# w1's parts loaded and transposed ahead of w_out, a sum of taps split around a tile, and softmax steps moved on ScalarE, in the start-up of a dynamic convolution with a max-out layer

## The chip, the cores and the metric

One core of one Trainium2 chip. The metric is the device time of one execution in microseconds (us), the median over several runs; lower is better. The engines are named as the profile names them: PE (TensorE, matmuls), PEld (its weight loads), DVE (VectorE), ACT (ScalarE), POOL (GpSimd), SP (SyncE, which here only issues DMAs). POOL issues DMAs too.

## The reference, cut to what matters

```python
# x (8, 4160, 192), weight_gen (8, 4160, 8 heads, 7 taps), all float32
w = exp(weight_gen - max); w = w / (sum(w over taps) + 1e-9)      # softmax over 7 taps
x_pad = zeros(6 rows) + x along the sequence
y[b, s, h, :] = sum over k of w[b, s, h, k] * x_pad[b, s + k, h, :]   # 24 channels a head
x2 = y.reshape(33280, 192)
h1 = x2 @ w1; h2 = x2 @ w2                                        # (192, 1024) each
out = maximum(h1, h2) @ w_out                                     # (1024, 192)
```

## The kernel before, in words

**Algebra.** maximum(h1, h2) is h1 + relu(h2 - h1). So the kernel keeps `wd` = w2 - w1 in bf16 for the hidden layer, and a small matrix `w10` = w1 @ w_out for the part without the relu. `w10` is a product that PE makes once (`w10_product`, lines 751 to 762): 8 matmuls with the transposed first 128 rows of w1 (part "E", line 755), then 16 with 64 columns each, which alternate between E and the transposed last 64 rows (part "T", line 759). The transposed parts lie in `w1t`; each is loaded and cast to bf16 by a DMA of POOL (lines 708 and 710) and transposed by a DMA of SP (line 713) that waits for that load. ACT copies the product out of PSUM (lines 766 and 768, `w10_copies`). `wo` is w_out in bf16, loaded by POOL (line 704), first read by the output matmuls of line 402 and then by the product.

**Layout.** The 33280 rows stand as 128 partitions of 260 columns. Columns are taken in batches of 16 (the last has 4). Of a batch, ACT makes exponentials of the logits (`exp_sum`, line 162), DVE their sums (`red`, 180), ACT the logarithms of the sums (`ln`, 186), DVE subtracts them from the logits (`shift`, 191), ACT makes the normalized weights (`weights(b, o)`, 202, o the first column in the batch; in batches 0 and 1 in pieces of 4 columns, two instructions each), and DVE multiplies x by them for all seven taps (`mul(b, o)`, 218, or `mul_pair`, 227) into `m_t`. From batch 2 on DVE adds the taps (`adds`, 244 to 253) and SP transposes the sums `yt` by a DMA (262). In batches 0 and 1, PE adds and transposes at once: `sum_part` (307) makes 84 matmuls of a piece of 4 columns against the identity, in two halves of 42, and ACT copies the result to `yt` (316). `sum_transpose` is both halves, with its copy at once or handed back (`features`).

**Hidden and output layer.** The 130 hidden tiles (1024 numbers in each partition) are made by `hid_tile` (362) and go through ACT's `relu` (372) to bf16. The output matmuls take wo with relu's result (402) and w10 with yt (415, in the start-up 457); ACT copies two or four columns' outputs to `o_t` (`evac`, 487), which SP stores (501). The tiles go in groups: of two up to tile 16 (so groups 0 to 7), of three from there. From group 3 on `hidden` writes out a group: hidden tiles, first half of the outputs of earlier columns, relus, second half, evac, and between them the softmax steps and sums of taps of later columns. A PSUM buffer of two tiles lets tile t + 2 begin when the relu of tile t is done.

**Order.** The schedule is written by hand: each engine runs its instructions in the order of the program text and waits by semaphores, so an instruction that waits holds all that stand behind it on its engine. `behind(first, load)` holds a load back until the instruction `first` is done, and with it all that stands behind the load on POOL. `relay` puts an empty instruction on a queue that waits for PE and that PE then waits for; the first (`out_hidden_only`, 440) is on SP, behind the transposes of w1.

The order around the change: groups 0 to 3 are written out one by one at lines 727 to 800; then `weights(1, 8)` (983), `rest_of_1` (807: the multiply of columns 8 to 11 of batch 1), and the loop over groups. In group 4 the exponential and sums of batch 2 stand behind the second relu (992), `weights(1, 12)` and `ln(2)` behind the output copy (905).

Of the kernel before, what the change touches and what calls it, by code (L numbers as in the profile page):

```python
# [23 lines left out]
def kernel(  # L24
# [9 lines left out]
    nc = tc.nc  # L34
# [3 lines left out]
    F = moe_w1.shape[1]  # L38
    P = 128
# [3 lines left out]
    HF = F // 2  # L43
# [65 lines left out]
    def load_wg(b, eng, o=0, n=None):  # L109
        c0, w = BATCHES[b]  # L110
        if b not in wg_ts:
            wg_ts[b] = pwg.tile([P, w * WGC], FP32, name="wg_t", tag="wg")
        parts = [(o, n)] if n else [(0, 8), (8, 8)] if c0 + w == LAST else [(0, w)]
        for o, n in parts:
            load = eng.dma_start(
                out=wg_ts[b][:, o * WGC:(o + n) * WGC],
                in_=bass.AP(tensor=weight_gen.tensor, offset=actual(c0 + o) * WGC,
                            ap=[[CPP * WGC, P], [1, n * WGC]]),
            )
        return load  # L120
# [9 lines left out]
    def load_x(b, o, n, halo=True):  # L130

        t, at = x_at(b, o)
        load = nc.gpsimd.dma_start(  # L133
            out=t[:, at + PAD * D:at + (PAD + n) * D],
            in_=bass.AP(tensor=x.tensor, offset=actual(BATCHES[b][0] + o) * D,
                        ap=[[CPP * D, P], [1, n * D]]),
        )
        if 0 < b < NB - 1 and o == 0 and halo:
            load_halo(b)
        if "wrap" in xb_ts and t is xb_ts["wrap"]:  # L140
            nc.gpsimd.memset(t[0:1, 0:PAD * D], 0.0)
            nc.gpsimd.dma_start(
                out=t[1:P, 0:PAD * D],
                in_=bass.AP(tensor=x.tensor, offset=(CPP - PAD) * D, ap=[[CPP * D, P - 1], [1, PAD * D]]),
            )
        return load
# [35 lines left out]
    def ln(b, i=0, of=1):  # L182
        if i == 0:
            s_ts[b] = psm.tile([P, BATCHES[b][1] * H], FP32, name="ln_t", tag="ln")
        hs = part(b, i, of)[0]
        nc.scalar.activation(out=s_ts[b][:, hs], in_=sums(b, hs), func=AF.Ln)  # L186
# [7 lines left out]
    def weights(b, o):  # L194

        w = dict(pieces(b))[o]
        if b not in en_ts:
            en_ts[b] = pen.tile([P, 16 * WGC * 2], BF16, name="en_t", tag="en")
        J = 2 if w == 4 and b < 2 else 1
        N = w * H // J  # L200
        for j in range(J):
            nc.scalar.activation(  # L202
                out=_sub(en_ts[b], (o * WGC + j * N * K) * 2, [[2 * N, K], [2, N], [1, 2]]),
                in_=_sub(wg_ts[b], (o * H + j * N) * K, [[1, K], [K, N], [0, 2]]), func=AF.Exp,
            )


    def mul(b, o):

        n = dict(pieces(b))[o]  # L210
        t, at = x_at(b, o)
        if n == 4 and b < 2:
            m_out = _sub(m_t, K * o * D, [[64, 2], [P, K * 6], [1, 64]])
            x_in = _sub(t, at, [[2 * D, 2], [D, K], [1, 2 * D]])
        else:
            m_out = m_t[:, K * o * D:K * (o + n) * D]
            x_in = _sub(t, at, [[D, K], [1, n * D]])
        return nc.vector.tensor_tensor(  # L218
            out=m_out, in0=x_in,
            in1=_sub(en_ts[b], o * WGC * 2, [[2, K * n * H], [0, G // 2], [1, 2]]),  # L220
            op=ALU.mult,
        )
# [56 lines left out]
    def half(j):  # L279
        return slice(64 * j, 64 * j + 64)  # L280
# [4 lines left out]
    def sum_transpose(u, taps=range(K), amid=lambda: None, now=True):  # L285

        copy = sum_part(u, 0, 3, taps)
        amid()
        sum_part(u, 3, 6, taps)
        if now:  # L290
            copy()
        return copy
# [30 lines left out]
    relu_of, yt_of, w10_of = {}, {}, []  # L323

    def behind(first, load):

        tc.add_manual_dep(load.ins, first.ins.name, SYNC, reason="its place among the transfers")
# [26 lines left out]
    def hid_tile(t):  # L354


        u = TILES[t][0]
        fs, w = chunks(t)
        for f in fs:
            for s in range(3):  # L360
                for j in range(2):
                    nc.tensor.matmul(  # L362
                        hid_out(t, f, j), lhsT=wd_at(j, s, f // 4, f % 4 * P, P),
                        rhs=_sub(yt_ts[u][half(j), :], (s + j) % 3 * P, [[3 * P, w // P], [1, P]]),
                        start=(f == fs[0] and s == 0), stop=(f == fs[-1] and s == 2),
                        skip_group_check=True,
                    )

    def relu(rd, t0, n):

        (hd, at), k = hd_at[t0], rd_at[t0][1]
        relu_of[t0] = nc.scalar.activation(out=rd[:, k * 1024:(k + n) * 1024], in_=hd[:, at:at + n * 1024],  # L372
                                           func=AF.Relu)
# [146 lines left out]
    OUTS, c = [[], [], []], 0  # L520
# [31 lines left out]
    def hidden(g, now=(), between=lambda: None, beside=lambda: None, ahead=lambda: None, amid=lambda: None):  # L552


        t0, n = GROUPS[g]
        rd = room(g)
        for t in range(t0, t0 + n - 1):
            hid_tile(t)
        if now:
            out_room(now, "ab" if n == 1 and "ab" in ps else None)  # L560
            last = out_first(now)
        if len(now) > 2:
            relu(rd, t0, n - 1)
        else:
            for t in range(t0, t0 + n - 1):
                relu(rd, t, 1)
        if now:
            go = relay(last)
        amid()
        hid_tile(t0 + n - 1)  # L570
        if len(now) > 2:
            beside()
        relu(rd, t0 + n - 1, 1)
        ahead()
        if now:
            out_second(now, go)
            evac(now[0] // 2, len(now) // 2)
        between()
        if len(now) <= 2:
            beside()  # L580
# [35 lines left out]
    with tc.tile_pool(name="pstage", bufs=1) as pstage:  # L616
# [73 lines left out]
        def halves_swapped(frm, bank):  # L690
# [10 lines left out]
        behind(first_exp, load_x(0, 4, 4))  # L701
        behind(first_mul, load_x(0, 8, 4))
        load_x(0, 12, 4)
        nc.gpsimd.dma_start(
            out=wo[:, :].rearrange("p (f d) -> p f d", d=D),
            in_=bass.AP(tensor=moe_w_out.tensor, offset=0, ap=[[D, P], [P * D, FCH], [1, D]]),
        )
        nc.gpsimd.dma_start(out=w1["E"], in_=bass.AP(tensor=moe_w1.tensor, offset=0, ap=[[F, P], [1, F]]))
        for h in range(2):
            nc.gpsimd.dma_start(out=w1["T"][half(h), :], in_=bass.AP(  # L710
                tensor=moe_w1.tensor, offset=P * F + h * HF, ap=[[F, 64], [1, HF]]))
        for kind, c0, w in (("E", 0, F), ("T", F, HF)):
            nc.sync.dma_start_transpose(out=w1t[:, c0:c0 + w].rearrange("p (b t) -> p b t", t=P), in_=w1[kind])
        mul_pair(0, 4, 0, 0, 4)
        sum_transpose(0, amid=lambda: halves_swapped(0, warm[:, 512:1024]))
# [18 lines left out]
        exp_sum(1)  # L734
        relu(rd, 1, 1)
        red(1)
        features = sum_transpose(1, now=False)
        weights(0, 8)
        mul(0, 8)
        features()  # L740
        rd = room(1)
        hid_tile(2)
        relu(rd, 2, 1)
        ln(1)
        shift(1)
# [18 lines left out]
        def w10_copies(pw):  # L764

            nc.scalar.copy(out=_sub(w10, 0, [[D, 2], [1, D]]), in_=_sub(pw, 0, [[512, 2], [1, D]]))
            for to, frm, at in ((64, 0, 0), (0, 64, 512)):
                w10_of.append(nc.scalar.copy(out=w10[to:to + 64, 2 * D:3 * D],
                                             in_=pw[frm:frm + 64, at:at + D]))
# [22 lines left out]
        weights(1, 4)  # L792
        mul(1, 4)
        relu(rd, 7, 1)
        w10_copies(pw)
        behind(w10_of[-1], load_wg(3, nc.gpsimd))
        load_halo(2)
# [8 lines left out]

    def rest_of_1():
        mul(1, 8)

    def end_of_1():  # L810
        mul(1, 12)
# [86 lines left out]
    def rest_of_sum(u):  # L898
        sum_part(u, 3, 6)
        begun[u]()  # L900
# [1 line left out]
    early = {  # L902
        3: (none, rest_of_1),
        4: (lambda: (behind(relu_of[8], load_x(2, 0, 8, halo=False)),
                     rest_of_sum(4), weights(1, 12), behind(yt_of[4], load_wg(4, nc.gpsimd)), ln(2)), end_of_1),
        5: (lambda: (exp_sum(3), red(3), sum_transpose(5, LEFT), weights(2, 0)), none),
        6: (lambda: (weights(2, 8), ln(3), rest_of_sum(6)), none),
        7: (lambda: (behind(relu_of[14], load_x(2, 8, 8)), rest_of_sum(7)), none),
# [71 lines left out]
            extra(t)  # L980

    evac(OUTS[3][0] // 2, len(OUTS[3]) // 2)
    weights(1, 8)
    early[3][1]()
    for g in range(4, len(GROUPS)):
        if GROUPS[g][1] == 3 and "c" not in ps:
            later_ps()
        tiles = [t for t in range(GROUPS[g][0], sum(GROUPS[g])) if t >= 16]
        if g == 9:
            behind(relu_of[16], load_x(3, 0, 8))  # L990
        if g in early:
            hidden(g, OUTS[g], early[g][0], ahead=lambda: (exp_sum(2), red(2)) if g == 4 else None,
                   amid=lambda: first_of_sum(g) if g != 5 else None)
            early[g][1]()
            steps(g, tiles)
        else:
            hidden(g, OUTS[g], beside=lambda: steps(g, tiles))
# [35 lines left out]
```

## Time and profile before

| | us |
|---|---|
| median of 3 runs | 413.52 |
| range of the runs | 412.25 to 414.07 |
| the profiled execution | 411.89 |
| its span (first to last instruction) | 410.1 |
| PE, DVE, ACT, POOL busy in the span | 396.3, 377.3, 353.8, 80.5 |

The profile is one execution, in us from the span's start. Busy time counts instructions on an engine; a wait is idle time, put down to what ended it (the releaser). In the timeline a row is a start, a duration, the engine, the line, the operation with output and inputs, the shape and the count, and in brackets the idle time ahead of it and its releaser; "DMA a<-b" as releaser is a transfer from b to a, "issue" is idle time in which the profile shows no wait. A row of the DMA issues gives the transfer, the queue that issued it, the count, the size of one and the median us from its issue to its landing. PE's granted clock was 0.99 or 1.00 in every stage.

### The profile page before, as it was taken

Reading aid. Unit: us, or ns where it says so; the run is one execution under the profiler, and the core shown is the slowest. Engines: PE = TensorE matmul, PEld = TensorE weight load, DVE = VectorE, ACT = ScalarE, POOL = GpSimd, SP = SyncE. Lnnn points to the kernel's source line nnn. Section 1 sums busy time; section 2 is a strip of 40 time slices with the busy share of each in tenths; the row PEclk is TensorE's granted clock in tenths of the full one; section 3 lists DMA queues with packets and bytes.
Section 4 is the critical chain, followed back from the end, with each engine's and each line's share of the span. In section 5 each row is a group of like instructions: output and inputs, shape, how many; then the busy total and the mean of one; then the engine's idle time right before and its main releaser. Section 6 shows DMA issues by size and latency. Waiting matters only on the chain.

```text
span 410.1 us, 16187 instructions
## 1 busy us (share of the span) xinstructions
PE 396.3 (97%) x7406; PEld 316.6 (77%) x7406; DVE 377.3 (92%) x230; ACT 353.8 (86%) x418; POOL 80.5 (20%) x108
## 2 busy tenths in 40 slices
PE   7779899999999999999999999999999999999995
PEld 2579899777777777777777778777777777777795
DVE  6997999999999999999999999999999999999500
ACT  3869999999989998898998999998999889898772
POOL 1412013122221112221210221222122223110000
PEclk9999999999999999999999999999999999999999
DMA  8987297757658774875785588477568657835323
GB/s 251 251 166 186 69 186 169 192 134 181 145 112 191 197 169 95 253 198 64 240 200 109 111 233 203 78 224 199 108 123 233 158 103 216 178 85 153 102 78 121
DMA packets 65110, 66.32 MB, mean 162 GB/s; under 512 B 49425, under 2 KB 54161, under 8 KB 65040
## 3 DMA queue, kind: packets, MB, share of 16 engines
q1 hardware_dynamic: 56064, 40.54, 35.8%
q0 software_dynamic: 8832, 24.63, 29.7%
q8 instruction: 58, 0.95, 0.9%
q10 hardware_dynamic: 144, 0.10, 0.1%
q14 instruction: 12, 0.10, 0.1%
HBM read 37.33 MB, written 25.56 MB: 153 GB/s over the span
## 4 chain that ended last, share of the span: by engine, by line
PE 85%; ACT 6%; issue 4%; DVE 1%; DMA 1%; POOL 0%; ACTq 0%; POOLq 0%; DVEq 0%
PE op_ps L402 38%; PE hd L362 38%; PE op_ps L415 7%; ACT rd_t L372 4%; DMA wg_t<-in_weight_gen_dram 1%; ACT en_t L202 1%; DVE m_t L227 1%; PE yps L307 1%; ACT yt L316 1%; DVE wg_t L191 0%; ACT e_t L162 0%; ACT o_t L487 0%; PE hdp L362 0%; ACT xb_t L150 0%; ACT ln_t L186 0%
## 5 line engine op out<-in xcount | busy, mean ns | idle before, releaser
L372 ACT ACTIVATE rd_t<-hd 128x1024 bf16<-128x1024 f32 (+1 forms) x206 | 234.5, 1187 | 26.3 <-PE hd L362 25.0
L402 PE MATMUL op_ps<-wo,rd_t 64*128 64x192 bf16 x4160 | 210.5, 243 | 0.0
L402 PEld LDWEIGHTS <-rd_t 64*128 64x128 bf16 x4160 | 180.8, 94 | 15.5
L362 PE MATMUL hd<-yt,wd 64*128 64x512 bf16 (+1 forms) x1584 | 187.3, 360 | 0.4 <-ACT rd_t L372 0.4
L218 DVE TENSOR_TENSOR m_t<-xb_t,en_t 128x10752 bf16<-128x10752 bf16 (+1 forms) x35 | 181.6, 5193 | 2.9 <-ACT en_t L202 2.8
L362 PEld LDWEIGHTS <-wd 64*128 64x128 bf16 x1776 | 94.2, 94 | 44.2 <-issue 2.7
L270 POOL CAST gate<-yt 128x1 f32<-128x1 bf16 x29 | 41.5, 1431 | 258.1 <-DMA yt<-y_t 258.1
L244 DVE TENSOR_TENSOR m_t<-m_t 128x4608 bf16<-128x4608 bf16 (+1 forms) x30 | 74.1, 2472 | 0.1
L487 ACT COPY o_t<-op_ps 128x384 f32<-128x384 f32 (+1 forms) x99 | 57.1, 588 | 12.5 <-PE op_ps L402 12.5
L415 PE MATMUL op_ps<-w,yt 64*128 64x192 bf16 x768 | 54.6, 243 | 0.5 <-ACT o_t L487 0.4
L415 PEld LDWEIGHTS <-yt 64*128 64x128 bf16 x768 | 37.7, 94 | 17.1 <-issue 1.6
L250 DVE TENSOR_TENSOR m_t<-m_t 128x3072 bf16<-128x3072 bf16 (+1 forms) x29 | 50.0, 1724 | 0.1
L202 ACT ACTIVATE en_t<-wg_t 128x896 bf16<-128x896 f32 (+2 forms) x45 | 35.8, 818 | 0.8 <-DVE wg_t L191 0.7
L253 DVE TENSOR_TENSOR y_t<-m_t 128x1536 bf16<-128x1536 bf16 (+1 forms) x29 | 27.3, 942 | 0.5
L133 POOL DMA_DIRECT2D xb_t<-in_x_dram x34 | 18.2, 536 | 30.6 <-ACT rd_t L372 19.9
L191 DVE TENSOR_TENSOR wg_t<-wg_t,ln_t 128x280 f32<-128x280 f32 (+5 forms) x46 | 22.2, 482 | 0.4 <-ACT ln_t L186 0.3
L372 ACT ACTIVATE rd_t<-hdp 128x1024 bf16<-128x1024 f32 x16 | 16.2, 1033 | 2.0 <-PE hdp L362 2.0
L162 ACT ACTIVATE e_t<-wg_t 128x896 f32<-128x896 f32 (+2 forms) x18 | 16.3, 903 | 1.4 <-DMA wg_t<-in_weight_gen_dram 1.4
L180 DVE TENSOR_REDUCE s_rest<-e_t 128x64 f32<-128x448 f32 (+2 forms) x27 | 16.3, 605 | 0.0
L362 PE MATMUL hdp<-yt,wd 64*128 64x256 bf16 x192 | 13.5, 269 | 2.4 <-issue 1.1
L477 DVE COPY o_last<-op_ps 128x192 f32<-128x192 f32 x1 | 0.4, 357 | 16.6 <-ACT o_last L477 16.6
L307 PE MATMUL yps<-ident,m_t 64*128 64x64 bf16 x636 | 11.7, 190 | 1.2 <-ACT yt L316 1.2
(53 smaller groups left out, 87.8 us busy)
## 6 DMA issues: line engine op xcount, KB each, us to landing
out_dram<-o_t SPq DMA_DIRECT2D x22, 768.0 KB, 5.2
xb_t<-in_x_dram POOLq DMA_DIRECT2D x30, 384.0 KB, 5.0
out_dram<-o_t SPq DMA_DIRECT2D x20, 384.0 KB, 3.1
wg_t<-in_weight_gen_dram POOLq DMA_DIRECT2D x13, 448.0 KB, 6.3
xb_t<-xb_t POOLq DMA_DIRECT2D x15, 288.0 KB, 5.3
xb_t<-in_x_dram POOLq DMA_DIRECT2D x4, 192.0 KB, 5.5
xs<-in_x_dram SPq DMA_DIRECT2D x1, 576.0 KB, 3.8
ws0E<-in_moe_w_dram SPq DMA_DIRECT2D x2, 256.0 KB, 5.6
```

The costliest lines, as they stand in the source:

```text
L191: nc.vector.tensor_tensor(out=w_t, in0=w_t, in1=_sub(s_ts[b], hs.start, [[1, hs.stop - hs.start], [0, K]]), op=ALU.subtract)
L202: nc.scalar.activation(out=_sub(en_ts[b], (o * WGC + j * N * K) * 2, [[2 * N, K], [2, N], [1, 2]]), in_=_sub(wg_ts[b], (o * H + j * N) * K ...
L218: return nc.vector.tensor_tensor(out=m_out, in0=x_in, in1=_sub(en_ts[b], o * WGC * 2, [[2, K * n * H], [0, G // 2], [1, 2]]), op=ALU.mult,)
L244: nc.vector.tensor_tensor(out=taps(0, 1, 3), in0=taps(0, 1, 3), in1=taps(3, 1, 3), op=ALU.add)
L250: nc.vector.tensor_tensor(out=taps(0, 2, 2), in0=taps(0, 2, 2), in1=taps(1, 5, 2), op=ALU.add)
L253: nc.vector.tensor_tensor(out=_sub(y_ts[b], o * D, [[64, 2], [P, 3 * w // 2], [1, 64]]), in0=taps(0, 1, 1), in1=taps(2, 1, 1), op=ALU.add,)
L270: nc.gpsimd.tensor_copy(out=gate, in_=yt[:, 0:1])
L362: nc.tensor.matmul(hid_out(t, f, j), lhsT=wd_at(j, s, f // 4, f % 4 * P, P), rhs=_sub(yt_ts[u][half(j), :], (s + j) % 3 * P, [[3 * P, w // ...
L372: relu_of[t0] = nc.scalar.activation(out=rd[:, k * 1024:(k + n) * 1024], in_=hd[:, at:at + n * 1024], func=AF.Relu)
L402: return nc.tensor.matmul(op_out(c), lhsT=rd[half(r), k * 1024 + at:k * 1024 + at + P], rhs=wo[half(r), f * D:(f + 1) * D], start=start, s ...
L415: nc.tensor.matmul(op_out(c + j), lhsT=yt_ts[u][half(j), (3 * i + (s + j) % 3) * P:(3 * i + (s + j) % 3 + 1) * P], rhs=w10[half(j), s * D: ...
L487: nc.scalar.copy(out=_sub(o, c % 24 * D, [[D, len(qs)], [h * D, 2], [1, D]]), in_=_sub(tile_, at + (qs[0] - p) * D, [[D, len(qs)], [512, 2 ...
```

## The change

Four edits, all in the first 50 us:

- POOL loads T, then E, then wo (before: wo, E, T), and SP transposes T ahead of E.
- The second sum of taps (piece 1 of batch 0) is split: its first half stays ahead of hidden tile 2, its second half and ACT's copy of it come behind that tile. The weights and the multiply of columns 8 to 11 of batch 0 keep their places on ACT and DVE, ahead of the copy.
- On ACT, `weights(1, 8)` moves from behind the first output copy to ahead of the copies of w10, `weights(1, 12)` and the exponential of batch 2 move from inside group 4 to ahead of its relus. DVE's order does not change: the sums of batch 2 follow the multiply of columns 8 to 11 in both.
- `ln(2)` stays where it was in group 4.

```diff
         load_x(0, 12, 4)
+        for h in range(2):
+            nc.gpsimd.dma_start(out=w1["T"][half(h), :], in_=...)
+        nc.gpsimd.dma_start(out=w1["E"], in_=...)
         nc.gpsimd.dma_start(out=wo[:, :].rearrange("p (f d) -> p f d", d=D), in_=...)
-        nc.gpsimd.dma_start(out=w1["E"], in_=...)
-        for h in range(2):
-            nc.gpsimd.dma_start(out=w1["T"][half(h), :], in_=...)
-        for kind, c0, w in (("E", 0, F), ("T", F, HF)):
+        for kind, c0, w in (("T", F, HF), ("E", 0, F)):
             nc.sync.dma_start_transpose(out=w1t[:, c0:c0 + w]..., in_=w1[kind])
...
-        features = sum_transpose(1, now=False)
+        features = sum_part(1, 0, 3)
         weights(0, 8)
         mul(0, 8)
-        features()
         rd = room(1)
         hid_tile(2)
+        sum_part(1, 3, 6)
+        features()
         relu(rd, 2, 1)
...
         relu(rd, 7, 1)
+        weights(1, 8)
         w10_copies(pw)
...
     def rest_of_1():
         mul(1, 8)
+        red(2)
...
-                     rest_of_sum(4), weights(1, 12), behind(yt_of[4], load_wg(4, nc.gpsimd)), ln(2)), end_of_1),
+                     rest_of_sum(4), behind(yt_of[4], load_wg(4, nc.gpsimd)), ln(2)), end_of_1),
...
     evac(OUTS[3][0] // 2, len(OUTS[3]) // 2)
-    weights(1, 8)
+    weights(1, 12)
+    exp_sum(2)
     early[3][1]()
...
-            hidden(g, OUTS[g], early[g][0], ahead=lambda: (exp_sum(2), red(2)) if g == 4 else None,
+            hidden(g, OUTS[g], early[g][0],
                    amid=lambda: first_of_sum(g) if g != 5 else None)
```

More of the change, by code (lines that the diff above doesn't have):

```diff
@@ L703 @@
         load_x(0, 12, 4)
+        for h in range(2):
+            nc.gpsimd.dma_start(out=w1["T"][half(h), :], in_=bass.AP(
+                tensor=moe_w1.tensor, offset=P * F + h * HF, ap=[[F, 64], [1, HF]]))
+        nc.gpsimd.dma_start(out=w1["E"], in_=bass.AP(tensor=moe_w1.tensor, offset=0, ap=[[F, P], [1, F]]))
         nc.gpsimd.dma_start(
@@ L707 @@
         )
-        nc.gpsimd.dma_start(out=w1["E"], in_=bass.AP(tensor=moe_w1.tensor, offset=0, ap=[[F, P], [1, F]]))
-        for h in range(2):
-            nc.gpsimd.dma_start(out=w1["T"][half(h), :], in_=bass.AP(
-                tensor=moe_w1.tensor, offset=P * F + h * HF, ap=[[F, 64], [1, HF]]))
-        for kind, c0, w in (("E", 0, F), ("T", F, HF)):
+        for kind, c0, w in (("T", F, HF), ("E", 0, F)):
             nc.sync.dma_start_transpose(out=w1t[:, c0:c0 + w].rearrange("p (b t) -> p b t", t=P), in_=w1[kind])
```

## The prediction

> **What bounds the kernel now.** First PE's waits from 15 to 50 us and from 50 to 405 us, and DVE's from 15 to 50; then the table by stage.
>
> ```profile
> PE pw L759 <- DMA w1t<-w1T: 2.1, 1, 2.1
> PE yps L307 <- ACT yt L316: 1.2, 2, 0.7
> PE hdp L362 <- issue: 1.1, 1, 1.1
> PE hdp L362 <- ACT rd_t L372: 1.0, 2, 0.7
> PE op_ps L415 <- ACT o_t L487: 0.4, 1, 0.4
> ```
>
> ```profile
> PE hd L362 <- ACT rd_t L372: 0.4, 2, 0.3
> ```
>
> ```profile
> DVE m_t L218 <- ACT en_t L202: 2.8, 2, 2.2
> ```
>
> ```profile
> 25.00:30.00 5.00, 2.86 (x53) 2.32 (x49) 5.00 (x2) 2.30 (x4) 0.00 (x0) 1.00 0.67 163
> 45.00:50.00 5.00, 4.26 (x149) 3.96 (x142) 5.00 (x3) 4.39 (x7) 0.53 (x1) 1.00 0.02 5
> 100.00:150.00 50.00, 50.00 (x864) 38.66 (x861) 49.93 (x30) 45.09 (x52) 10.22 (x12) 1.00 0.70 170
> ```
>
> (Waits: engine, line, releaser, total us, times, longest. Stages: PE, PEld, DVE, ACT, POOL busy, granted clock, DMA.) After 47.82 us, where PE resumes from its last start-up wait, PE is full until its last matmul at 405.8 us at a clock of 1.00. So the kernel is a start-up plus 358 us of PE that the change leaves alone; time is won or lost only by moving that 47.82, and then one for one. Before it PE stands 2.1 us at line 759, and DVE, also full later, loses 2.8 us. The timeline joins the two:
>
> ```profile
> 27.21 0.27 PE L759 MATMUL pw<-wo,w1t 128*64 128x192 bf16 x1
> 29.63 0.85 PE L759 MATMUL pw<-wo,w1t 128*64 128x192 bf16 x15 [2.14 <-DMA w1t<-w1T]
> ...
> 33.98 2.96 DVE L218 TENSOR_TENSOR m_t<-xb_t,en_t 128x5376 bf16<-128x5376 bf16 x1 [2.19 <-ACT en_t L202]
> ```
>
> PE waits for the transposed last rows of w1; ACT, in program order, waits 2.9 us for PE's product (its copies start at 30.51); the weights that DVE needs stand behind them on ACT, at 33.23.
>
> **Part 1, transfers.** Landing times, from the DMA issues between 10 and 30 us:
>
> ```profile
> wo<-in_moe_w_out_dram POOLq DMA_DIRECT2D x1, 384.0 KB, 7.4
> xb_t<-xb_t POOLq DMA_DIRECT2D x1, 288.0 KB, 5.8
> w1E<-in_moe_w_dram POOLq DMA_DIRECT2D x1, 256.0 KB, 7.8
> w1T<-in_moe_w_dram POOLq DMA_DIRECT2D x2, 64.0 KB, 7.5
> w1t<-w1E SPq DMA_TRANSPOSE x1, 4.3
> w1t<-w1T SPq DMA_TRANSPOSE x1, 7.2
> ```
>
> With POOL's issues at 11.45, 12.34, 12.87 and 13.39 us, wo lands at 18.85, E at 20.1, T at 20.9: one queue, in order, E costing 1.3 and T 0.7 us behind wo. The x part ahead of them (issued 10.93) lands at 17.05. In the new order T lands at 17.8, E at 19.1, wo at 20.9; the bytes, and x behind them, are as before. SP issues T's transpose at 17.8 (1.19 us) and E's at 19.1 (2.13 us), free at 21.2; next on SP is the relay that PE waits for at 24.36, so nothing queues there. E's transpose lands 4.3 us after its issue, at 23.4; T's, even at 7.2, at 25.0. The product asks for E at 26.45 and T at 27.21, so both are there, and it ends at 27.27 + 0.85 = 28.12 instead of 30.48: 2.36 us off PE.
>
> The price is wo, first read at 21.77 (line 402). Its margin falls from 2.9 to 0.9 us, and the transposes now run beside it. Their DMA time:
>
> ```profile
> q1 hardware_dynamic: 1056, 0.26, 82.5%
> q0 software_dynamic: 108, 0.34, 39.2%
> ```
>
> ```profile
> q0 software_dynamic: 109, 0.33, 101.9%
> q1 hardware_dynamic: 1, 0.00, 0.1%
> ```
>
> (Packets, MB and share of the DMA engines from 21 to 24 us, then from 24 to 26; queue 1 is SP's, 0 POOL's.) E needed 82.5% of 3 us = 2.5 us; T, by the same reckoning in 26 to 28 (32.3%), 0.65. Bounds for wo: 20.9, if queued loads go first, as x did over T from 24 us (T was issued at 22.43); 24.0, if both transposes go first, as E did from 21 us. T comes 0.65 us long in wo's middle and E's packets start 1 us after issue, at wo's tail, so I take the middle, 22.3: PE stands 0.5 us (0 to 2.2) at 21.77 and the product ends at 28.6.
>
> The Trainium skill (DMA: Bandwidth & Descriptors, "Queues, rings and completion order") says each DMA engine takes turns between rings packet by packet. The 109 to 1 does not look like turns. By that rule wo would land near 22.4, the stall would be 0.65, and the forecast would stay.
>
> **Part 2, ACT.** weights(1, 8) takes ACT's idle after the relu that ends at 27.57: two instructions, 0.71 us, done by 28.3 (28.8 with the stall), in cover that is 0.55 us or more; at worst the copies of w10 start 0.2 us late. DVE's multiply of columns 8 to 11 then follows its addition (line 244, to 31.80) at once instead of at 33.98: 2.18 us. Its x landed at 27.0. From the product's end P, ACT runs copies (1.15), yt (done P+2.2), the first output copy (P+2.05 to 2.87), weights(1, 12) (from P+2.74), exp_sum(2) (0.94, from P+3.34; its logits landed at 30.1), then the two relus of group 4. Moving these ahead puts 1.5 us before those relus, less the 0.6 us of weights(1, 8) that left: the first ends at P+5.2 instead of P+4.4. PE needs it at P+5.75 (36.24), so this is hidden by 0.5 us; every us beyond would be PE's. What comes back is behind the relus: output copy to P+6.5 instead of P+6.93 removes PE's 0.4 us at L415; yt ends at P+7.2; ln(2) could start at P+7.1.
>
> DVE now decides: multiply 31.80 to 34.78, red(2) (1.09) to 35.88, so ln(2) at 35.9. With P = 28.6 ACT is there at 35.7: the 0.5 us stall on wo is absorbed. Then on ACT ln (0.2 to the next), two relus (0.92 each), copy (0.37), exponential (0.84), yt (0.83) end at 39.95 where before they ended at 42.64; the next sum of taps starts at 39.97 instead of 42.69. DVE: mul(1, 12) to 38.84, shift(2) to 39.87; weights(2, 0) starts 39.9 instead of 42.73, 2.83 us sooner. The row of ACT pieces from there to 47.78 has no gap, so it moves whole, and PE resumes at 44.99. Its waits agree: 2.36 + 0.40 go, 1.2 stays. Loads that the relus release (x of batch 2: 6.4 us to landing, after the relu at 33.8) land at 40.2, its multiply starts at 41.0; 0.8 us of cover.
>
> **Part 3, the sum around tile 2.** 42 of the 84 matmuls move behind 12 of the tile's. The tile's matmuls ran from 17.20 (idle marked "issue") and their relu from 18.30; ACT has no idle from 15 to 24 us, and its order there is the same. Zero; at most 0.3 us, if the yt copy has to wait for the tile, and as much the other way.
>
> **Sum.** 2.8 us sooner (2.18 + 0.65 on the DVE and ACT chain): span 410.1 to 407.3; the profiled execution, 411.89 with 1.8 us around the span, to 409.1. It lies 1.6 us under the median of the runs, 413.52; the same 2.8 off the median is 410.7. Measurement can tell 0.5% (2.1 us) from no change; the three runs spread over 1.8 us.
>
> **The rivals.**
> 1. *wo comes last* (24.0, transposes ahead): P = 30.3, ACT reaches ln(2) at 37.4, 1.5 us behind DVE, so the gain is 1.3: 412.2. For it: 1056 packets to 108. Against: wo is queued 5 us earlier than E's transpose.
> 2. *The stall moves from T to E.* E is now the second transpose, and the product asks for it first. If it is passed by the x load of 22.25 (landed 27.0), as T was, it starts near 26.3 and lands at 29.0; the product takes 1.7 us, so P is 30.7. DVE's 2.2 us is won, but from P on ACT is the bound: yt ends at P+11.2 = 41.9 against 42.64: gain 0.7, 412.8. Against: E is issued 3 us before that load, and landed in 4.3 us beside another.
> 3. *Slower by the same place*: E takes T's fate whole and falls behind the logits' load too. T landed at 29.58; E's DMA time is 1.85 us more, so 31.4; P = 33.1, gain 42.64 - 11.2 - P = -1.7: 415.2. It decides from P = 31.45, E landing after 29.7. For it: T took 7.2 us for half the data; against: E would need 12.3.
> 4. *Given back later*: a new wait of PE on ACT (90% busy; the two waits of 0.4 us above) or on loads eats it: 413.5. Against: DVE, ACT and PE move together, and batch 2's yt landed 10 us ahead of use (61.8 against 71.8).
> That the change does not do what it says is ruled out by the built order: DVE's is unchanged, ACT's, POOL's and SP's are as described.
>
> **How the numbers follow.** Forecast 0.61, rivals 0.13, 0.11, 0.07, 0.08. Range: the bottom is the forecast with 0.9 of the 1.2 us of waits that stay gone too, 409.8; the top, 413.6, takes in rivals 1, 2 and 4; rival 3 and tails, under 0.2, stay out. Faster by 0.5% (under 411.45): 0.85 of the forecast and a sixth of rival 1, 0.54; slower (over 415.6): half of rival 3 and a little spread, 0.06; same 0.40.
>
> **What would show it.** Right: no wait on w1t; at most 0.7 us at line 402's first wo; DVE's wait on en_t gone; PE's resumption near 45 us; 358 us after it. Wrong: a wait for wo over 1 us, a wait at line 756 for E, the wait for yt near 45 us longer than 0.7, or new PE waits after 50 us.

## The result, and the profile after

| | before | after |
|---|---|---|
| median, us | 413.49 | 410.64 |
| range of the runs | 411.87 to 415.55 (14 runs) | 410.14 to 411.80 (14 runs) |
| ratio after to before | | 0.9935 (0.9917 to 0.9952) |
| the profiled execution | 411.89 | 411.17 |
| its span | 410.1 | 409.4 |

The kernel is 0.65% faster, 2.85 us by the medians. The two profiled executions differ by 0.7 us only: that of before lies 1.6 us under its median, that of after 0.5 us above its own. What follows reads the profiles for the mechanism and the medians for the size. A ratio, here and below, leaves out single runs far above the rest of their kernel, so it can lie nearer to 1 than two medians do.

PE's waits from 15 to 50 us in the kernel after (engine, line, releaser, total us, times, longest):

```profile
PE hdp L362 <- ACT rd_t L372: 1.5, 2, 1.2
PE yps L307 <- issue: 1.1, 3, 0.5
PE yps L307 <- ACT yt L316: 0.5, 1, 0.5
PE op_ps L402 <- issue: 0.4, 1, 0.4
```

The wait for `w1t` is gone, and so are ACT's waits behind it but one. New are four pieces of idle time marked "issue", 1.57 us together. DVE's waits in the same stretch:

```profile
DVE s_rest L180 <- ACT e_t L162: 0.8, 1, 0.8
DVE m_t L218 <- ACT en_t L202: 0.5, 1, 0.5
```

The 2.19 us ahead of the multiply of columns 8 to 11 are gone; two smaller waits have come later, both for ACT. The timeline of PE, from the product to its last start-up wait, with DVE's multiply:

```profile
26.90 0.83 PE L756 MATMUL pw<-wo,w1t 128*128 128x192 bf16 x8
27.66 0.85 PE L760 MATMUL pw<-wo,w1t 128*64 128x192 bf16 x16
28.44 0.37 PE L307 MATMUL yps<-ident,m_t 64*128 64x64 bf16 x13
29.33 1.21 PE L307 MATMUL yps<-ident,m_t 64*128 64x64 bf16 x71 [0.52 <-issue]
30.37 0.67 PE L457 MATMUL op_ps<-w,yt 64*128 64x192 bf16 x12
30.87 0.82 PE L362 MATMUL hdp<-yt,wd 64*128 64x256 bf16 x12
31.52 0.42 PE L415 MATMUL op_ps<-w,yt 64*128 64x192 bf16 x6
31.77 0.83 PE L402 MATMUL op_ps<-wo,rd_t 64*128 64x192 bf16 x16
32.43 0.34 PE L307 MATMUL yps<-ident,m_t 64*128 64x64 bf16 x11
33.06 0.62 PE L307 MATMUL yps<-ident,m_t 64*128 64x64 bf16 x31 [0.30 <-issue]
...
46.74 0.79 PE L307 MATMUL yps<-ident,m_t 64*128 64x64 bf16 x42 [0.46 <-ACT yt L316]
```

```profile
32.16 2.95 DVE L218 TENSOR_TENSOR m_t<-xb_t,en_t 128x5376 bf16<-128x5376 bf16 x1
```

The product's 24 matmuls run without a gap (lines 756 and 760 are 755 and 759 of before). PE then stops in the middle of a sum of taps, where no semaphore is waited for. Between the first two of these gaps lie 71 + 12 + 12 + 6 + 16 + 11 = 128 matmuls, each with its weight load: 256 PE instructions. The next two gaps (at 37.34 and 42.16 us) follow after 128 matmuls each. The last start-up wait ends at 46.74 us, where it was 47.82. The transfers:

```profile
wo<-in_moe_w_out_dram POOLq DMA_DIRECT2D x1, 384.0 KB, 8.5
w1t<-w1T SPq DMA_TRANSPOSE x1, 6.6
w1t<-w1E SPq DMA_TRANSPOSE x1, 5.9
```

wo, issued at 12.98, lands at 21.51, 0.7 us ahead of its first reader (22.22). T's transpose lands at 24.89, E's at 25.69, both ahead of the product at 26.90. After 50 us PE's only wait is the 0.4 us at line 362 that was there before.

From the resumption to PE's last matmul it is 357.97 us in both profiles. It stays within 0.2 us of this in every further profile but two: one is 0.8 us longer (experiment 7), and the one with other sums of taps (8) is not counted. So PE's resumption (the sum of taps that waits for the sixth `yt` of the loop) is the figure to compare. The spans say less: from PE's last matmul to the end of the span it is another 4.1 to 5.5 us in these profiles (4.3 before, 4.7 after).

**What "issue" is here.** Counted from PE's first instruction, matmuls and weight loads together, the four gaps lie ahead of instructions 961, 1217, 1473 and 1729. Before has one, of 1.13 us, ahead of 449. All are 449 + 256n. To each belongs one 16384-byte packet of the DMA queue that the profile calls "instruction" (26.94, 30.78, 35.01 and 39.80 us in the kernel after, about 0.9 us long). PE goes on 1.3 to 1.5 us after the packet's end. There are 58 such packets for PE's 14,812 matmuls and weight loads, one for every 256. So PE waits for its own program; experiments 3 and 9 test this. The Trainium skill (Runtime: NRT & Kernel Launch, "Instruction fetch mechanics") says that instructions come in 16 KiB blocks of 256, fetched while the block before is executed, at a cost that is mostly hidden. The trace agrees with the size of the block and, in the start-up, not with the hiding: here a block costs PE 0.3 to 0.5 us, in before's case 1.1.

### The profile page after: what moved, and what is told of

It is laid out like the page before. It is cut to its first block, busy times and chain, and to the rows that moved or that the text cites. A ratio compares the mean times of both kernels' runs of the same rounds, so it can differ in the third digit from the quotient of the medians.

```text
span 409.4 us, 16186 instructions
## 1 busy us (share of the span) xinstructions
PE 398.0 (97%) x7406; PEld 317.0 (77%) x7406; DVE 377.2 (92%) x230; ACT 353.8 (86%) x418; POOL 81.2 (20%) x108
## 4 chain that ended last, share of the span: by engine, by line
PE 89%; ACT 6%; DMA 1%; issue 1%; SPq 1%; DVE 0%; ACTq 0%
PE op_ps L402 40%; PE hd L362 38%; PE op_ps L415 7%; ACT rd_t L372 3%; PE hdp L362 2%; PE yps L307 2%; DMA ws1T<-in_moe_w_dram 1%; ACT yt L316 1%; ACT e_t L162 0%; ACT o_t L487 0%; SPq L642 0%; ACT en_t L202 0%; SPq L625 0%; ACT xb_t L150 0%; SPq L634 0%
## 5 line engine op out<-in xcount | busy, mean ns | idle before, releaser
L253 DVE TENSOR_TENSOR y_t<-m_t 128x1536 bf16<-128x1536 bf16 (+1 forms) x29 | 27.3, 941 | 0.5
```

The costliest lines, as they stand in the source:

```text
L253: nc.vector.tensor_tensor(out=_sub(y_ts[b], o * D, [[64, 2], [P, 3 * w // 2], [1, 64]]), in0=taps(0, 1, 1), in1=taps(2, 1, 1), op=ALU.add,)
```

## The experiments

Three questions. Which edit carries the gain: the transfers, ACT's moves or both (experiments 1 to 6). What ate the part of it that the profile of after lacks: instruction fetches, or ACT again (7 to 9). And what made T late in before: a race between SP's transpose of T and POOL's load of x's columns 8 to 15 of batch 1 (`load_x(1, 8, 8)`), the one issued first going first, or a second transpose that is slow in any case (10 to 12).

The table gives every timed kernel. "Stretch" is PE's time from the start of the matmuls of tile 5 to the resumption, which leaves out that executions reach tile 5 at 20.5 to 21.5 us. Ratios are to the kernel before as it ran beside each, whose median stands next to them.

| kernel | median (range), us | before | ratio, interval | stretch |
|---|---|---|---|---|
| before, two profiles | | | | 27.31, 27.33 |
| after, with the result | 410.64 (410.14 to 411.80) | 413.49 | 0.9935 (0.9917 to 0.9952) | 25.78 |
| transfers alone | 410.57 (409.95 to 411.86) | 412.52 | 0.9958 (0.9928 to 0.9987) | 25.48 |
| ACT's moves alone | 411.95 (408.86 to 415.22) | 412.52 | 0.9982 (0.9946 to 1.0018) | 24.86 |
| split sum alone | 411.96 (410.29 to 414.83) | 412.52 | 1.0005 (0.9969 to 1.0041) | 28.99 |
| after, E before T | 410.82 (409.89 to 411.73) | 412.52 | 0.9961 (0.9935 to 0.9988) | 25.84 |
| after, again | 411.18 (410.68 to 411.88) | 412.78 | 0.9970 (0.9945 to 0.9995) | 25.98 |
| transfers alone, again | 411.42 (411.08 to 412.89) | 412.78 | 0.9995 (0.9976 to 1.0015) | 26.10 |
| after, later exponential | 411.11 (410.47 to 417.34) | 412.78 | 0.9986 (0.9960 to 1.0012) | 24.93 |
| after, sums in half the matmuls | 419.31 (417.87 to 422.66) | 412.78 | 1.0205 (1.0162 to 1.0247) | |
| before, x load later | 410.20 (409.30 to 412.60) | 413.76 | 0.9936 (0.9909 to 0.9964) | 24.90 |
| after, 4 more warm-up matmuls | 411.19 (410.36 to 412.16) | 413.76 | 0.9948 (0.9915 to 0.9981) | 26.83 |
| after, x load later | 410.87 (410.07 to 412.70) | 412.76 | 0.9950 (0.9924 to 0.9976) | 25.71 |

**1. The transfers alone.**

```diff
+        for h in range(2):
+            nc.gpsimd.dma_start(out=w1["T"][half(h), :], in_=...)
+        nc.gpsimd.dma_start(out=w1["E"], in_=...)
         nc.gpsimd.dma_start(out=wo[:, :].rearrange("p (f d) -> p f d", d=D), in_=...)
-        nc.gpsimd.dma_start(out=w1["E"], in_=...)
-        for h in range(2):
-            nc.gpsimd.dma_start(out=w1["T"][half(h), :], in_=...)
-        for kind, c0, w in (("E", 0, F), ("T", F, HF)):
+        for kind, c0, w in (("T", F, HF), ("E", 0, F)):
```

> Only the order of w1's and wo's loads and of the two transposes is changed; the sum of taps and ACT's order stay as before. My theory: PE's wait at line 759 goes, the product ends near 28.1 us, weights(1, 8) still stands 2.7 us behind it on ACT but is then done at 31.6, no later than DVE is free (31.80); ln(2) comes at 36.2 instead of 35.9. So 2.4 us sooner than before (0.4 us less than the whole change), no wait of PE on w1t, at most 0.3 us of DVE on en_t at the multiply of columns 8 to 11. Rival, that the moves on ACT make the gain: within 0.5 us of before.

Measured: 410.57 us, 1.95 under before's median. No wait for `w1t`. PE's waits for ACT of before stay (0.39, 0.46 and 0.72 us), and there is one fetch gap of 0.21 us behind tile 5. The edit by itself gives about what the whole change gives.

**2. ACT's moves alone.**

```diff
         relu(rd, 7, 1)
+        weights(1, 8)
         w10_copies(pw)
...
         mul(1, 8)
+        red(2)
...
-                     rest_of_sum(4), weights(1, 12), behind(yt_of[4], load_wg(4, nc.gpsimd)), ln(2)), end_of_1),
+                     rest_of_sum(4), behind(yt_of[4], load_wg(4, nc.gpsimd)), ln(2)), end_of_1),
...
-    weights(1, 8)
+    weights(1, 12)
+    exp_sum(2)
...
-            hidden(g, OUTS[g], early[g][0], ahead=lambda: (exp_sum(2), red(2)) if g == 4 else None,
+            hidden(g, OUTS[g], early[g][0],
```

> Only ACT's order is changed (two weights and an exponential); loads, transposes and the sum stay as before. My theory: PE still waits about 2.1 us for the last rows of w1; DVE's 2.2 us gap at the multiply of columns 8 to 11 goes, but ACT, which starts from the product's end, binds: 0.7 to 1.0 us sooner than before. Rival, that DVE's gap is what counts: 2 us or more sooner.

Measured: 411.95 us, ratio 0.9982 (0.9946 to 1.0018), which cannot be told from no difference. The profile caught an execution without the race: SP issued T's transpose at 22.70, POOL the x load at 23.08; T landed at 28.09, and PE did not wait for it although nothing was done about the transfers. Behind tile 5's start PE waits for ACT no more; in the start-up it has two fetch gaps (0.31 us ahead of 449, 0.69 ahead of 1473). The runs spread over 6.4 us, and the fastest, 408.86, is the lowest of the study. So T's lateness may be a matter of which of two issues 0.4 us apart comes first, and this profile says nothing of what ACT's moves bring while PE does wait for T.

**3. The split sum alone.**

```diff
-        features = sum_transpose(1, now=False)
+        features = sum_part(1, 0, 3)
...
-        features()
...
         hid_tile(2)
+        sum_part(1, 3, 6)
+        features()
```

> Only the second sum of taps is split around hidden tile 2. My theory: nothing, within 0.3 us of before, since ACT has no idle time from 15 to 24 us and its order is the same. Second statement, on the idle time marked issue: in both profiles PE stands idle with no wait shown ahead of its rows 449 (before), 961, 1217, 1473 and 1729 (after), all of the form 449 + 256 n, so I take it for the fetch of the next 256 instructions; in this kernel row 449 lies in the sum and no longer in the tile, so the tile's matmuls should run at about 16 us instead of 17.2. If the idle time belongs to the tile's own waits, they still run at 17.2.

Measured: 411.96 us, no difference (ratio 1.0005). Tile 2's matmuls start at 15.71 instead of 17.20 us and the gap ahead of instruction 449 is gone, but PE then waits for relus and reaches tile 5 at 20.74, not sooner. Here the x load went first (22.48 against 22.67), and the wait is back:

```profile
PE pw L760 <- DMA w1t<-w1T: 2.2, 1, 2.2
```

The stretch of this profile, 29.0 us, is 1.7 longer than before's, though PE's waits in it are nearly the same (3.84 us against 3.72). The rest, 1.6 us, is PE's clock. From 30 to 35 us the stage reads, here and then in before (the granted clock is the number ahead of the last two):

```profile
30.00:35.00 5.00, 5.00 (x131) 4.61 (x133) 1.78 (x2) 2.87 (x6) 1.08 (x2) 0.66 0.32 68
```

```profile
30.00:35.00 5.00, 5.00 (x197) 4.72 (x195) 2.77 (x3) 4.12 (x8) 1.08 (x2) 1.00 0.37 88
```

In steps of 1 us it is 0.50 from 31 to 34 us, just behind the wait for T, and the 84 matmuls of a sum take 2.26 us there instead of 1.40. The mean granted clock of each run says that this is frequent in the kernel before: of its 97 runs beside the experiments (those that count in the ratios) 44 have 0.996 or less, with a median of 413.97 us; the other 53 have a median of 411.74. With ACT's moves or the split alone 9 of 23 runs have so low a clock. Of the 113 runs of the kernels that load w1's parts ahead of wo, or x later, none has. So the lower clock goes with the old order of transfers; before's two profiles, however, have the wait and no drop, a run's mean does not say when its clock was low, and what sets the drop off is not shown.

**4. The change with E ahead of T.** POOL's loads as E, T, wo, and SP's transposes in that order.

> The changed kernel, but E is loaded and transposed first and T second (both still ahead of wo). My theory: the order of the two does not matter once both are ahead of wo: T's transpose is issued near 21 us and lands by 26, the product asks for T at 27.6; time within 0.3 us of the changed kernel. Rival, that the second, smaller transpose is passed by the x load of 22 us as it was before: T lands at 27.5 to 29.5, PE waits up to 2 us at line 760 and up to 1.5 us of the gain goes.

Measured: 410.82 us, as the change itself within its range. E's transpose landed at 24.74, T's at 25.24. The order of the two does not matter once both are issued by 20.1 us.

**5 and 6. The change and the transfers alone, side by side again.** No new edit.

> The changed kernel once more, on the chip of the three kernels beside it. Theory: 410.5 us, runs within 2 us of each other, where those of the kernel before spread over 4 us or more, since their wait for T hangs on whether SP issues T's transpose ahead of POOL's x load of 22 us or behind it (22.43 against 22.25 in the profile of before, 22.67 against 22.48 with only the sum split, both with the wait; 22.70 against 23.08 with only ACT's order changed, without it).

> Only the transfers' order changed, beside the whole change on the same chip. My working of the prediction: 0.4 us slower than the whole change. Theory now, from the idle time of 1.6 us in all at PE's rows 961, 1217, 1473 and 1729 in the whole change against 0.2 us here: PE cannot pass 256 instructions in less than some 4 us in the start-up, so what ACT's new order frees is lost to that, and the two are equal within 0.3 us.

Measured: 411.18 and 411.42 us. ACT's moves bring 0.24 us by the medians, less than either spread, and 0.28 by the resumption (46.73 against 47.01). Where the changed kernel stands 0.69 and 0.61 us for instructions 1473 and 1729, the one without ACT's moves stands 0.39 and 0.20 us for ACT at the two places next to them, and 0.74 instead of 0.46 us at the last. Against the kernel before, the transfers alone have the ratio 0.9995 (0.9976 to 1.0015) here, where experiment 1 had 0.9958: this second comparison by itself shows no gain. That the transfers carry it rests on the first, and on the resumptions, 47.02 and 47.01 us against 47.82 and 48.03.

**7. Taking ACT's last two waits away.** The exponential of batch 3 moves ahead of a relu, the sixth `yt` copy ahead of weights(2, 8) and ln(3).

```diff
-        5: (lambda: (exp_sum(3), red(3), sum_transpose(5, LEFT), weights(2, 0)), none),
-        6: (lambda: (weights(2, 8), ln(3), rest_of_sum(6)), none),
+        5: (lambda: (red(3), sum_transpose(5, LEFT), weights(2, 0)), none),
+        6: (lambda: (rest_of_sum(6), weights(2, 8), ln(3)), none),
-                   amid=lambda: first_of_sum(g) if g != 5 else None)
+                   amid=lambda: first_of_sum(g) if g != 5 else exp_sum(3))
```

> The changed kernel, with two more moves on ACT: the exponential of batch 3 goes ahead of the second relu of group 5, into an idle stretch of 0.9 us, and the copy of the sum of piece 6 goes ahead of weights(2, 8) and ln(3), so that PE's 0.46 us wait for that copy goes. By the order of ACT and DVE alone it is 0.8 to 1.0 us sooner than the changed kernel. If PE's fetch of instructions is the limit of the start-up, under 0.4 us, with longer idle times at rows 1729 and 1985.

Measured: 411.11 us against 411.18 of the change beside it. The wait for `yt` is gone and PE passes the resumption at 45.85, 0.88 us sooner. But 0.8 us come back by its last matmul: 358.75 us from there instead of 357.97. A gain on ACT's side is again not a gain of the kernel. Of the 0.8 us, 0.7 come back at two of the next fetches: ahead of instructions 2241 (49.3 us) and 2497 (55.8 us) two neighbouring matmuls start 0.43 and 0.31 us apart, in the changed kernel beside it 0.02. Both are 449 + 256n, one and more blocks behind the rows that I had named.

**8. The sums of taps in half as many PE instructions** (in the changed kernel; its lines stand one or two further up, and ACT's copy of the sums is adapted). 42 matmuls of 128 x 128 for a piece instead of 84 of 64 x 64, so that the fetches come at half the rate in the sums.

```diff
-                for r in range(2):
-                    nc.tensor.matmul(yps[:, r*512 + k*64:...], lhsT=m_t[half(r), at:at + P], rhs=ident[half(r), half(r)], ...)
+                nc.tensor.matmul(yps[:, k*P:(k + 1)*P], lhsT=m_t[:, at:at + P], rhs=ident[:, 0:P], ...)
```

> The changed kernel, with each sum of taps on PE made by 42 matmuls over 128 partitions and 128 columns instead of 84 over 64 partitions and 64 columns: half the instructions of a sum (84 fewer weight loads and matmuls), at about 1.1 us more PE time for each sum of 84 by the columns (0.43 ns a column). If the idle time without a shown wait is the fetch of each next 256 instructions, it goes (under 0.4 us in all), and the time is within 1 us of the changed kernel, PE's own time paying for it. If it belongs to something else in the start-up, it stays and the time rises by 2 us or more.

Measured: 419.31 us, 2% slower; my expectation of the time was wrong. The gaps did go: from 15 to 50 us PE's only wait is

```profile
PE hdp L360 <- ACT rd_t L370: 1.3, 2, 1.1
```

but the sums cost more on PE than the gaps had. The matmuls of the sums over the whole span, in the kernel before and in this one (count, busy us, mean ns of one):

```profile
L307 PE MATMUL yps<-ident,m_t 64*128 64x64 bf16 x636 | 11.7, 190 | 1.2 <-ACT yt L316 1.2
```

```profile
L306 PE MATMUL yps<-ident,m_t 128*128 128x128 bf16 x318 | 20.2, 219 | 0.1
```

Half as many, and 8.5 us more of busy time; the median is 8.1 us above that of the changed kernel beside it (411.18). Half a piece takes 1.28 us instead of 0.62. That no gap is left fits the theory, though a slower PE gives every fetch more time as well.

**9. Four more warm-up matmuls at PE's start**, in the changed kernel, so that all later instructions have a number 8 higher.

```diff
-        keep_warm(18)
+        keep_warm(22)
```

> The changed kernel with 22 instead of 18 warm-up matmuls at PE's start: each of them is a weight load and a matmul, so every later PE instruction has a number 8 higher. Theory of the instruction fetch (PE stops where the next 256 instructions have not arrived): the idle times marked issue come 4 matmuls earlier in the same groups of instructions, still at numbers 449 + 256n, each 0 to 0.7 us, and PE's sum of such gaps between 17 and 45 us stays 1 to 2 us. Rival (the gaps belong to the instructions where they stand, through a wait that the profile does not show): they stay at the same matmuls of the sums of taps, at numbers 8 higher. Time within 0.6 us of the changed kernel in both.

Measured: 411.19 us, and the gaps moved as the theory says, from the 14th matmul of the sum to the 10th:

```profile
28.18 0.32 PE L307 MATMUL yps<-ident,m_t 64*128 64x64 bf16 x9
29.34 1.26 PE L307 MATMUL yps<-ident,m_t 64*128 64x64 bf16 x75 [0.84 <-issue]
```

The other three lie 4 matmuls earlier too, all ahead of 961, 1217, 1473 and 1729 again. Their sum, 2.44 us, is above the 1 to 2 I had expected. A wait that belongs to a place in the program would have stayed there; this one belongs to the instruction's number.

**10. Before, with the x load one relu later.**

```diff
         relu(rd, 4, 1)
-        behind(relu_of[4], load_x(1, 8, 8))
         hid_tile(5)
         relu(rd, 5, 1)
+        behind(relu_of[5], load_x(1, 8, 8))
```

> The kernel before with one edit: POOL's load of x's columns 8 to 15 of batch 1 is held until the relu of tile 5 (it was the relu of tile 4), so that T's transpose is issued ahead of it. Theory of the race (T's wait arises when that load is issued before SP's transpose of T): the load comes near 24 us, T's transpose near 22.5, T lands by 28.1 at the latest (as in the run with ACT's moves alone), PE's wait for T at line 759 is under 0.5 us; DVE's multiply of columns 8 to 11 is still held by the weights behind the copies, but those come up to 2 us sooner; time 410.8 to 412, and its runs spread over no more than 2.5 us against some 5 to 9 of the kernel before. Rival (T is slow because the transposes stand in one queue, whatever x does): T's transpose lands 7 us after its issue again, the wait stays near 2 us, the time stays at the kernel before's median (412.5 to 413.5). A load of x that is late by about 1.5 us lands near 28.5, ahead of the multiply that reads it (32 us or later) in both.

Measured: 410.20 us, ratio 0.9936 (0.9909 to 0.9964): this one line gives what the four edits give, better than I expected. T's transpose was issued at 22.21 and landed 4.4 us later, at 26.61, 0.66 us ahead of its reader; the load was issued at 23.23. PE's waits:

```profile
PE hdp L362 <- ACT rd_t L372: 1.3, 2, 1.1
PE yps L307 <- ACT yt L316: 1.0, 2, 0.7
PE hdp L362 <- issue: 0.8, 1, 0.8
PE op_ps L415 <- ACT o_t L487: 0.4, 1, 0.4
```

The rival (a second transpose is always slow) falls. The waits for ACT are before's own, and the one fetch gap is that ahead of 449; behind tile 5 there is none. None of its 12 runs has a mean clock under 0.997. The runs spread over 3.3 us, more than the 2.5 expected.

**11. A further profile of before.**

> A further profile of the kernel before, unchanged. Theory of the race: if the load of x (columns 8 to 15 of batch 1) is issued ahead of T's transpose, T lands 6 us or more after its issue and PE waits 1.5 us or more at line 759; if it is issued behind it, T lands 5.5 us after its issue and the wait is under 0.5 us. Rival: the wait is near 2 us in either order. PE's gaps marked issue: at number 449 (1 us), and at most one other.

Measured: 412.22 us, a single execution. The transpose of T and the x load were issued in the same hundredth (22.44); T landed at 29.80, PE waited 2.17 us, and the resumption was at 48.03. Its gap marked issue lies ahead of 449. So with four profiles of before's order of loads: load first or level, T lands 7.2 to 7.4 us after its issue (before, the split, this one); transpose first by 0.38 us, 5.4 us.

**12. The change with the x load one relu later.** The edit of 10 in the changed kernel.

> The changed kernel with POOL's load of x's columns 8 to 15 of batch 1 held until the relu of tile 5, as in the run of the kernel before with that one edit. Both transposes are issued well ahead of that load in any case, so the race for T is no issue here. Theory (PE's start-up is now limited by instruction fetches, which came 1 us after PE reached the block in that run and 3 us after it in the changed kernel): the fetch near 27 us comes near 25, PE's gap at number 961 and those behind it shrink from 1.6 us in all to under 0.8, and PE resumes near 45 us: ratio to the kernel before 0.990 to 0.993, some 409.5 us. Rival (the fetches come when they come, or PE then waits for ACT at the same places as the one-line kernel did, 0.4, 0.3 and 0.7 us): no better than the two kernels alone, ratio 0.993 to 0.996, 410.2 to 411.

Measured: 410.87 us, no better than either alone, as the rival had it. The gap at 961 shrinks to 0.18 us, and the one at 1729 grows to 0.88; with 0.30 at 1217 they make 1.36 us together, beside 0.35 us for `yt`.

## Why the prediction was right, and where it was not

The forecast, 410.7 us, faster by 2.8, is met in the median, 410.64. Its steps were not all met.

- **A start-up plus 358 us.** Held to 0.2 us in nearly every kernel here.
- **T off PE.** The product was to end 2.36 us sooner, at 28.1 without a stall; it ended at 28.5, and tile 5 had started 0.45 us later in this execution. T's and E's transposes landed at 24.89 and 25.69 (25.0 and 23.4 expected): E's took 5.9 us, not 4.3. The margin was still 1.2 us, so rivals 2 and 3 are out.
- **wo.** Landed at 21.51, between the lower bound (20.9) and my middle (22.3). The 0.5 us stall did not come, and rival 1 is out. The 22.4 us that the prediction worked out by turns between rings (the Trainium skill, DMA: Bandwidth & Descriptors, "Queues, rings and completion order") was 0.9 too late in this execution.
- **Part 2.** DVE's multiply followed its addition at once, at 32.16 (31.80 expected, 0.36 of it the late start). ln(2) ran at 36.35 (35.9), all of it the late start. From there the chain slipped: ACT waited 0.92 us for a hidden tile whose matmuls stand right behind PE's gap at 37.34 us, weights(2, 0) ran at 41.33 instead of 39.9, and PE resumed at 46.74 instead of 44.99.
- **Part 3.** Zero within what the split alone can tell (ratio 0.9969 to 1.0041).

The term that failed is "2.36 + 0.40 go, 1.2 stays". From tile 5 to the resumption PE waited 3.72 us in before (2.14 for T, 1.58 for ACT). After, it waited 2.03: 0.46 for ACT and 1.57 for instructions. The stretch shrank by 1.53 us instead of 2.83. I had taken the 1.13 us "issue" at tile 2 as a fixed cost of that place; it was the first of a series that shows wherever PE is not held up by something else. Rival 4 (given back later) had the right kind of event, but it looked for it on ACT and the loads, and after 50 us.

That the median still moved by 2.85 us comes from the other side. I took 2.8 us off the median as off the profile, but before's executions differ. One reason is T's race: stretches of 27.3 us where the load went first or level, 24.9 with T first (experiments 2 and 10). The other is PE's clock, for which the prediction has no term: the split alone, with before's loads, has 29.0 us, about 1.6 of it from a clock at half for some 3.4 us, and the 44 of before's 97 runs with a low mean clock have a median 2.2 us above the others' (experiment 3). Both profiles of before show the wait without the drop. The changed order of transfers has 25.5 to 26.1 us in five profiles (after, and experiments 1, 4, 5 and 6), 24.9 and 26.8 with the further edits of experiments 7 and 9. So the change buys safety from the bad cases and is, by the stretch, about 1 us slower than before's order at its luckiest. Two sizes were off in opposite ways, and the agreement to 0.1 us is partly luck: side by side again, the difference was 1.6 us. How often before's runs lose the race is not measured; only profiles show it.

Open is what sets the start of a fetch. In the kernel of experiment 10 the third packet came at 24.52 us, 1.0 us after PE had entered the block before; in the kernel after it came 3.1 us after. Delaying the x load in the changed kernel brought it to 26.17 only (2.8 us after). That the packet waits behind other transfers is possible and not shown.

## What to carry to other kernels

When a transfer lands late by chance, look at which of two queues issued first, and by how little: moving the competitor one step was worth as much here as reordering the loads, splitting a sum and moving work on ACT. Before taking a gap marked "issue" as fixed, count the engine's instructions up to it: where gaps lie 256 apart, they are instruction fetches, and shortening other waits turns into these. Judge a change in the start-up from several profiles: one execution may sit well off its median, and the same kernel may win or lose a race. And before putting a spread of runs down to a wait alone, compare the granted clock of the runs.

## What the runs showed of the hardware

- PE can run out of instructions. In the start-up it executes a block of 256 in 3.4 to 4.5 us between the gaps of after; the gaps are of 0.2 to 0.9 us, up to 1.1 ahead of 449. In each of them PE goes on 1.2 to 1.6 us after the end of the 16384-byte packet, and where the packet ended 2.8 us ahead (experiment 10, instruction 961) there is none. From the resumption on 12,815 matmuls and weight loads take 358 us, 7.2 a block, and no gap is left in the kernel after.
- In the old order, SP's transpose of T (two halves of 64 KB) took 4.4 us from issue to landing with the x load 1 us behind it, 5.4 with it 0.4 us behind, and 7.2 to 7.4 with it level or ahead. In the kernel after it took 6.6 us, issued at 18.32 us while two loads that POOL had issued earlier were still under way (landed at 21.51 and 23.50).
- PE's granted clock can fall to half in mid-run: in the profile of the split alone it is 0.50 from 31 to 34 us, behind a wait of 2.25 us for T that ended at 29.95, and 1.00 again from 35. Waits of 2.14 and 2.17 us at the same place in two other profiles had no such drop.
